# Layer 2's output product by Strassen's scheme, in one fused attention and two-layer MoE kernel

## The chip, the cores and the metric

The kernel runs on one core of a Trainium2 chip. The metric is device time in microseconds (us) for one execution. The kernel before took 905.86 us (median of 3 runs, 905.23 to 908.45). Engines: TensorE (PE; its weight loads are listed as PEld), VectorE (DVE), ScalarE (ACT), GpSimd (POOL) and SyncE (SP), which issues the DMAs one after the other. Matrix products accumulate in eight banks of PSUM.

## The reference

```python
attn_out = _attn_ref(q, k, v)                 # 4 x 8 heads x 576 x 64, causal window of 64
x = attn_out as (2304 tokens, 512)
# layer 1
xn = x / sqrt(mean(x*x) + 1e-6) * rms_g
g = xn @ w_gate;  h = g / (1 + exp(-g)) * (xn @ w_val)       # 512 x 1536 weights
x = h @ w_out                                                # 1536 x 512
# layer 2
gate = 1 / (1 + exp(-(x @ w2_gate)))
out = (gate * (x @ w2_val)) @ w2_out                         # (2304, 512)
```

All inputs and outputs are float32. A product is made of float16 parts: each operand is split into a high and a low part, and high x high, high x low and low x high are added up in PSUM, so that one product of a 128 x 128 weight piece is three matmuls.

## The kernel before

The 2304 tokens are six blocks of 384, and two blocks make a token pair (p = 0, 1, 2). The 1536 hidden columns are twelve tiles of 128 (f), and two tiles make a slab (s = 0 to 5). Weights come from DRAM in slabs j of 1 MB: j = 0 to 11 are gate and value (two for each hidden slab), j = 12 to 17 the output weights. A slab is loaded, its largest value is found (`w_max`), it is rounded (`w_conv`) and split into high and low part (`w_split`). For layer 2 a slab that was loaded early for its largest value is often loaded again later.

Already before the change, the gate and value products of layer 2 (all three pairs) and of pair 2 in layer 1 use Strassen's scheme (in Winograd's form) on 2 x 2 quadrants: `sums` makes the four weight combinations, which gives seven forms of a weight slab, `xform_items` makes seven forms of the tokens (four DVE subtractions, seven splits), and `moe_w(l, p, s)` runs seven products in place of eight for gate (m = 0) and seven for value (m = 1), each of six matmuls of 384 columns, and puts the quadrants together with ACT copies into PSUM banks and DVE adds (line 799). For layer 2 it then makes tanh (line 832), multiplies (line 840) and splits each of the four hidden quadrants into high and low part (ACT line 850, DVE line 851).

The output product of layer 2 is plain: `moe_o(1, blk, f)` runs, for each of the three 128-token tiles of a block, three matmuls of 512 columns (lines 636 to 638) with the hidden tile as the weight operand. After the last f, each token tile is scaled on ACT or DVE (lines 644, 646) and stored as 128 rows of 512 (line 648).

The seven token forms of a pair lie in `att` for pairs 0 and 2, and in places of `wl1` and `wl2` for pair 1 (`xform`). Layer 1's results `x2` stay in SBUF in the `xhl` buffers.

Program order is the list `main`: steps GV and W (gate and value), O (output product), with other work put beside them by `place`. The order in which each engine runs its instructions is then set wholly by the written list `ORDER`, unpacked in `arrange`: SP too takes its DMAs in that order. PSUM banks and buffers are taken from small lists (`room`, `take()`) in turn.

```python
for t in range(n // P):
    ts_ = slice(t * P, (t + 1) * P)
    T.matmul(o[t], lhsT=h[:, 0, ts_], rhs=wh, start=st, stop=False)
    T.matmul(o[t], lhsT=h[:, 0, ts_], rhs=wl, start=False, stop=False)
    T.matmul(o[t], lhsT=h[:, 1, ts_], rhs=wh, start=False, stop=en)
```

Of the kernel before, what the change touches and what calls it, by code (L numbers as in the profile page):

```python
# [35 lines left out]
CO = 6  # L36
AEND, REND = 7, 6
TRUNC = None
PLACE = {}
WIDE = set()  # L40
# [7 lines left out]
        10: (2, 28), 11: (2, 35), 12: (2, 42), 13: (2, 46), 14: (2, 50), 15: (1, 42), 16: (1, 48), 17: (1, 52)}  # L48
# [23 lines left out]
BANKS_OF = {"o": (0, 1, 2, 3), "gv": (4, 5), "at": (6, 7), "w": (4, 5, 6, 7), "any": (0, 1, 2, 3, 4, 5, 6, 7), "oat": (0, 1, 2, 3, 6, 7)}  # L72
# [35 lines left out]
def fused_kernel(ctx, tc, q, k, v, w_gate, w_val, w_out, rms_g, w2_gate, w2_val, w2_out, const16, const32, out, plan, asked):  # L108
# [5 lines left out]
    P = 128  # L114
# [15 lines left out]
    sp = Pool(ctx.enter_context(tc.tile_pool(name="sp", bufs=2)), plan, asked)  # L130
    ps = Pool(ctx.enter_context(tc.tile_pool(name="ps", bufs=1, space=bass.MemoryType.PSUM)), plan, asked)
# [88 lines left out]
    def wdst(layer, j):  # L220
        if layer == 0:
            return wl1[:, j * 2048:(j + 1) * 2048]
        home, k = DST2[j]
        return (wl1 if home == 1 else wl2)[:, k * KIB:(k + (7 if j < 12 else 4)) * KIB]
# [5 lines left out]
    def w_max(layer, j, n=1):  # L230
# [15 lines left out]
        top = 266 if layer == 1 and j < 12 else 268  # L246
# [45 lines left out]
    def w_l2_scale():  # L292
        pgv = pw[:, 1, 0:12].rearrange("p (s m) -> p s m", m=2)
        pf = small("pf", NG)
        V.tensor_tensor(out=pf, in0=pgv[:, :, 1], in1=pw[:, 1, 12:18], op=ALU.mult)
        cm = small("cm")
        V.tensor_reduce(out=cm, in_=pf, axis=AX.X, op=ALU.max)
        ic = small("ic")
        V.reciprocal(out=ic, in_=cm)
        V.tensor_scalar(out=hs2, in0=pf, scalar1=ic, scalar2=2.0 ** -21, op0=ALU.mult, op1=ALU.mult)  # L300
        V.tensor_scalar(out=tg2, in0=pgv[:, :, 0], scalar1=pt, scalar2=2.0 ** -39, op0=ALU.mult, op1=ALU.mult)
        V.tensor_scalar(out=ocm, in0=cm, scalar1=pt, scalar2=2.0 ** -32, op0=ALU.mult, op1=ALU.mult)
# [12 lines left out]
    def w_split(layer, j, half):  # L315
# [10 lines left out]
        if layer == 1 and j < 12:  # L326
            parts = [(x, d[:, 0:1024], d[:, 1792:2816]), (wraw(layer, j)[:, 0:768, 0].bitcast(F32), d[:, 1024:1792], d[:, 2816:3584])]
# [10 lines left out]

    def wo(layer, f):
        w = wdst(layer, 12 + f // 2)  # L340
        o = (f % 2) * 512
        return w[:, o:o + 512], w[:, 1024 + o:1536 + o]

# [260 lines left out]
    def moe_h(l, blk, f):  # L604
# [7 lines left out]
        hh[l, blk, f] = h  # L612
# [3 lines left out]
    def moe_o(l, blk, f):  # L616
        n = BLOCKS[blk]
        h = hh.pop((l, blk, f))
        if f == 0:
            ob[l, blk] = [bank("o") for _ in range(KC if l == 0 else n // P)]  # L620
        o = ob[l, blk]
        wh, wl = wo(l, f)
        st, en = f == 0, f == FC - 1
        if l == 0:
            hi, lo = h[:, 0, 0:n], h[:, 1, 0:n]
            for c in range(KC):
                cs = slice(c * P, (c + 1) * P)
                T.matmul(o[c][:, 0:n], lhsT=wh[:, cs], rhs=hi, start=st, stop=False)  # L628
                T.matmul(o[c][:, 0:n], lhsT=wh[:, cs], rhs=lo, start=False, stop=False)  # L629
                T.matmul(o[c][:, 0:n], lhsT=wl[:, cs], rhs=hi, start=False, stop=en)  # L630
            if (l, blk, f) in hbuf:
                room.append(hbuf.pop((l, blk, f)))
        else:
            for t in range(n // P):
                ts_ = slice(t * P, (t + 1) * P)
                T.matmul(o[t], lhsT=h[:, 0, ts_], rhs=wh, start=st, stop=False)  # L636
                T.matmul(o[t], lhsT=h[:, 0, ts_], rhs=wl, start=False, stop=False)  # L637
                T.matmul(o[t], lhsT=h[:, 1, ts_], rhs=wh, start=False, stop=en)  # L638
            room.append(hbuf.pop((l, blk, f)))
        if en and l == 1:  # L640
            for t in range(n // P):
                y = abuf("sm" if t % 2 else "vn", 0)
                if t % 2 == 0:
                    A.activation(out=y, in_=o[t], func=AF.Copy, scale=bx[blk // 2][2])
                else:
                    V.tensor_scalar(out=y, in0=o[t], scalar1=bx[blk // 2][2], scalar2=None, op0=ALU.mult)
                r0 = starts[blk] + t * P
                SY.dma_start(out=out[r0:r0 + P, :], in_=y)
            ob.pop((l, blk))
# [7 lines left out]
    def x1_a(blk):  # L657
        o = ob.pop((0, blk))
# [14 lines left out]
    sxs = {}  # L673
# [17 lines left out]
    def xform(l, p, q):  # L691
        if (l, p) == (1, 1):
            home, k = (wl1, 56 + 3 * q) if q < 5 else (wl2, 56 + 3 * (q - 5))
            a = home[:, k * KIB:(k + 3) * KIB]
        else:
            a = att[:, 2 * NMAX * q:2 * NMAX * (q + 1)].bitcast(F16)
        return a.rearrange("p (t k n) -> p t k n", t=2, k=2)

    def xform_items(l, p):
# [72 lines left out]
    def h5_home(f):  # L772
        s, i = divmod(f, 2)
        if s == 1:
            return abuf("sm", 0)[:, 0:NMAX]
        if s in (2, 3):
            if "x" not in h5:
                h5["x"] = six()
            return h5["x"][:, 2 * (s - 2) + i]
        o = {0: (40, 54), 4: (28, 29.5), 5: (31, 32.5)}[s][i]  # L780
# [6 lines left out]
    def product(pb, l, p, s, m, a, b, first):  # L787
        w, x = wdst(l, 2 * s + m), xform(l, p, b)
# [12 lines left out]
    def moe_w(l, p, s):  # L801
        be = bx[p][1][:, s:s + 1] if l else tgs[:, s:s + 1]
        th = {}
        for m in range(2):
# [13 lines left out]
            c = bank("w")  # L818
# [8 lines left out]
            for k, v in (((0, 0), a[:, 0:NMAX]), ((1, 1), x22), ((1, 0), x21), ((0, 1), c[:, 0:NMAX])):  # L827
# [13 lines left out]
                if held:  # L841
                    room.append(v)
                blk, f = 2 * p + j, 2 * s + i
                if not l and j:
                    hb = h5_home(f)
                else:
                    hb = hbuf[l, blk, f] = take()
                h = hb.bitcast(F16).rearrange("p (t n) -> p t n", t=2)
                sc = hs2[:, f // 2:f // 2 + 1] if l else 1.0
                A.activation(out=h[:, 0], in_=t, func=AF.Copy, scale=sc)  # L850
                V.scalar_tensor_tensor(out=h[:, 1], in0=t, scalar=sc, in1=h[:, 0], op0=ALU.mult, op1=ALU.subtract)
                hh[l, blk, f] = h
                room.append(t)


# [55 lines left out]
    late_o = [(b, f) for b in range(NB) for f in range(FC)]  # L911
    for p in range(NB // 2):
        for s in range(NG):
            main.append(("W", 1, p, s))
            for _ in range(4 if p else 2 if s else 0):
                oo(1, late_o[0][0], [late_o[0][1]])
                late_o.pop(0)
    for b, f in late_o:
        oo(1, b, [f])
# [27 lines left out]
    if True:  # L947
# [62 lines left out]
        lst += [load(12), load(13)] + conv(1, 12) + [load(14)] + conv(1, 13) + conv(1, 14)  # L1010
        for j in (4, 5, 6, 7, 8, 9, 10, 11, 15, 16, 17):
# [17 lines left out]
        after("W", 2, 5, [(("be",), lambda: x1_c(0))] + again(8, 9) + again(15))  # L1029
        after("O", 5, FC - 3, again(16, 17))  # L1030
# [19 lines left out]
        def do_o(l, b, f):  # L1050
            moe_o(l, b, f)
            if l == 0 and f == FC - 1:
                x1_a(b)

        def rooms():
# [3 lines left out]
            for i in range(2):  # L1059
                spare.append(abuf("vn", 0)[:, 0:NMAX])  # L1060
# [7 lines left out]
        def late_rooms():  # L1068
            for a in spare:
                k = [i for i, x in enumerate(room) if x is a]  # L1070
                room.pop(k[0])
            more_room(2)
            for home, k in ((wl2, 54), (wl1, 46)):
                room.append(home[:, k * KIB:k * KIB + 2 * NMAX].bitcast(F32))
# [200 lines left out]
```

## Time and profile before

| what | value |
|---|---|
| median of 3 runs | 905.86 us |
| the profiled execution | 904.97 us |
| its span | 903.2 us |
| PE, busy share of the span | 97% |
| DVE, busy share | 71% |
| ACT, busy share | 50% |
| DMA, mean rate | 84 GB/s |

The span runs from the first to the last recorded piece of work. A group of instructions is listed by its line and engine, with the tiles it writes and reads, the number of instructions, the engine's busy time in them and the mean duration of one. The chain of waits is followed back from the last instruction, at each step to what released it. Matmuls are pipelined, so their durations overlap; the distance of two starts is what one costs.

### The profile page before, as it was taken

The page shows a single profiled execution, that of the slowest core. Times are in us where ns is not written, and L with a number is a line of the kernel's source. Part 1 is how long each engine was busy: PE and PEld are TensorE (multiplying, and loading weights), DVE is VectorE, ACT ScalarE, POOL GpSimd, SP SyncE. Part 2 cuts the span into 40 slices and gives each one's busy share as a digit, 9 for nine tenths or more (in the row PEclk, how much of TensorE's full clock was granted, in tenths as well). Part 3 has the DMA queues.
Part 4 walks back from the last instruction along what each step waited for, and adds up shares of the span by engine and source line. Part 5 has one row for each costly group of instructions (what it writes and reads, how often), then busy time and mean ns, then how long its engine had stood idle before and what let it go on. Part 6 is the DMA issues. An engine that isn't in the chain of part 4 may idle for free.

```text
span 903.2 us, 14978 instructions
## 1 busy us (share of the span) xinstructions
PE 873.1 (97%) x6048; PEld 519.5 (58%) x6048; DVE 641.0 (71%) x1228; ACT 454.6 (50%) x965; POOL 30.8 (3%) x40
## 2 busy tenths in 40 slices
PE   4699999999999999999999999999999999999998
PEld 3566666666656666556666665555555555555543
DVE  6999998999999999999989577745342442223340
ACT  5867456547634555356565475454343432333420
POOL 0100000110020010100000000000000000000000
PEclk7799999999999999999999999999999999999999
DMA  9734534413684030001212122000000000000001
GB/s 345 276 135 167 205 129 165 158 65 118 226 309 159 13 106 25 1 1 48 94 48 94 47 94 94 1 1 1 24 12 1 24 1 1 36 1 36 1 35 47
DMA packets 19797, 75.44 MB, mean 84 GB/s; under 512 B 2320, under 2 KB 2704, under 8 KB 13712
## 3 DMA queue, kind: packets, MB, share of 16 engines
q1 hardware_dynamic: 19728, 74.49, 22.3%
q8 instruction: 47, 0.77, 0.3%
q14 instruction: 22, 0.18, 0.1%
HBM read 69.77 MB, written 4.72 MB: 82 GB/s over the span
## 4 chain that ended last, share of the span: by engine, by line
PE 78%; DVE 15%; DMA 4%; issue 1%; ACT 0%; POOL 0%; SPq 0%; DVEq 0%; ACTq 0%
PE bank L796 36%; PE bank L577 11%; PE bank L637 5%; PE bank L638 5%; PE bank L636 5%; PE bank L628 4%; PE bank L630 4%; PE bank L629 4%; DVE wmax L238 2%; DVE wl L332 2%; DMA wl<-in_moe_w_gate_dram 2%; DMA wl<-in_moe_w_out_dram 1%; PE bank L405 1%; PE bank L477 1%; DVE wl L267 1%
## 5 line engine op out<-in xcount | busy, mean ns | idle before, releaser
L796 PEld LDWEIGHTS <-wl 128*128 128x128 f16 x1944 | 190.2, 98 | 137.2 <-issue 1.2
L796 PE MATMUL bank<-att,wl 128*128 128x384 f16 x1440 | 252.6, 326 | 0.9 <-DVE att L709 0.9
L577 PE MATMUL bank<-xhl,wl 128*128 128x384 f16 x1152 | 197.4, 326 | 3.2 <-DVE th L590 1.7
L577 PEld LDWEIGHTS <-wl 128*128 128x128 f16 x1152 | 112.0, 98 | 77.5 <-issue 5.1
L809 ACT ACTIVATE bank<-bank 128x384 f32<-128x384 f32 x96 | 45.7, 476 | 121.3 <-PE bank L796 99.2
L330 ACT ACTIVATE wl<-wl,isc 128x1024 f16<-128x1024 f32 (+1 forms) x42 | 48.4, 1165 | 7.7 <-DVE isc L247 4.2
L589 ACT ACTIVATE th<-bank,tg 128x384 f32<-128x384 f32 x48 | 27.7, 576 | 44.8 <-PE bank L577 34.1
L421 ACT ACTIVATE sm<-sm,nm 128x128 f32<-128x128 f32 x96 | 37.3, 391 | 23.6 <-DVE nm L415 23.5
L238 DVE TENSOR_REDUCE wmax<-wl 128x1 f32<-128x1024 f32 x36 | 43.4, 1213 | 4.8 <-DMA wl<-in_moe_w_out_dram 2.0
L796 PE MATMUL bank<-wl 128*128 128x384 f16 x252 | 45.9, 326 | 0.0
L796 PE MATMUL bank<-wl,wl 128*128 128x384 f16 x252 | 45.2, 326 | 0.0
L265 ACT ACTIVATE wl<-wl 128x1024 f32<-128x1024 f32 x36 | 41.2, 1157 | 7.6 <-DMA wl<-in_moe_w_gate_dram 5.6
L636 PE MATMUL bank<-wl,xhl 128*128 128x512 f16 x111 | 42.1, 379 | 0.0
L637 PE MATMUL bank<-wl,xhl 128*128 128x512 f16 x111 | 42.1, 379 | 0.0
L638 PE MATMUL bank<-wl,xhl 128*128 128x512 f16 x111 | 42.1, 379 | 0.0
L840 DVE SCALAR_TENSOR_TENSOR xhl<-xhl,bank 128x384 f32<-128x384 f32 x18 | 9.9, 553 | 42.7 <-PE bank L796 42.7
L628 PE MATMUL bank<-wl,wl 128*128 128x384 f16 x120 | 39.2, 327 | 0.0
L629 PE MATMUL bank<-wl,wl 128*128 128x384 f16 x120 | 39.1, 326 | 0.0
L630 PE MATMUL bank<-wl,wl 128*128 128x384 f16 x120 | 39.1, 326 | 0.0
L630 PEld LDWEIGHTS <-wl 128*128 128x128 f16 x288 | 28.2, 98 | 18.6
L628 PEld LDWEIGHTS <-wl 128*128 128x128 f16 x288 | 28.1, 98 | 18.6 <-issue 1.0
L799 DVE TENSOR_TENSOR xhl<-xhl,bank 128x384 f32<-128x384 f32 x26 | 14.3, 552 | 34.3 <-PE bank L796 28.7
(339 smaller groups left out, 1540.3 us busy)
## 6 DMA issues: line engine op xcount, KB each, us to landing
wl<-in_moe_w_val_dram SPq DMA_DIRECT2D x16, 1024.0 KB, 5.0
wl<-in_moe_w_gate_dram SPq DMA_DIRECT2D x16, 1024.0 KB, 5.3
wl<-in_moe_w_out_dram SPq DMA_DIRECT2D x15, 1024.0 KB, 4.8
vn<-in_v_dram SPq DMA_DIRECT2D x27, 256.0 KB, 4.9
att<-in_k_dram SPq DMA_DIRECT2D x13, 384.0 KB, 5.4
att<-in_q_dram SPq DMA_DIRECT2D x17, 256.0 KB, 5.2
out_dram<-vn SPq DMA_DIRECT2D x12, 256.0 KB, 2.2
out_dram<-sm SPq DMA_DIRECT2D x6, 256.0 KB, 2.2
```

Of the source, the lines that this page charges most:

```text
L238: V.tensor_reduce(out=r1[:, i:i + 1], in_=wraw(layer, j + i)[:, :, 1].bitcast(F32), axis=AX.X, op=ALU.max, apply_absolute_value=True)
L265: A.activation(out=y.bitcast(F32), in_=hi.bitcast(F32), func=AF.Prelu, scale=2.0 ** -112, alpha=-2.0 ** 32)
L330: A.activation(out=hi, in_=y, func=AF.Copy, scale=sc)
L577: T.matmul(pb[:, 0:n], lhsT=w_, rhs=x_, start=(c == 0), stop=(c == m - 1))
L628: T.matmul(o[c][:, 0:n], lhsT=wh[:, cs], rhs=hi, start=st, stop=False)
L629: T.matmul(o[c][:, 0:n], lhsT=wh[:, cs], rhs=lo, start=False, stop=False)
L630: T.matmul(o[c][:, 0:n], lhsT=wl[:, cs], rhs=hi, start=False, stop=en)
L636: T.matmul(o[t], lhsT=h[:, 0, ts_], rhs=wh, start=st, stop=False)
L637: T.matmul(o[t], lhsT=h[:, 0, ts_], rhs=wl, start=False, stop=False)
L638: T.matmul(o[t], lhsT=h[:, 1, ts_], rhs=wh, start=False, stop=en)
L796: T.matmul(pb[:, 0:NMAX], lhsT=w_, rhs=x[:, t, kk], start=first and kk == n == 0, stop=kk == 1 and n == 2, skip_group_check=not first)
L809: A.activation(out=o[:, 0:NMAX], in_=i[:, 0:NMAX], func=AF.Copy)
```

## The change

- The output weights of layer 2 get Strassen forms as well: each of the slabs 12 to 17 now goes through `sums`, and its split covers 1792 columns in place of 1024.
- `moe_w` for layer 2 no longer splits four hidden quadrants; it makes seven forms of them (four DVE subtractions, seven splits on ACT and DVE).
- `moe_o` is left for layer 1 alone. The new `moe_p(p, ss, c)` runs layer 2's output product for one token pair, a group `ss` of two slabs, and one half c of 128 columns in each half of the output. It has seven products, each of 2 slabs x 3 matmuls of 384 columns, with the weight as weight operand, so that the result is transposed. The result of the first group goes from PSUM to an SBUF accumulator, those of the other two are added to it on DVE, and after the last group it is stored as 128 rows of 384. The host transposes the output array.
- Layer 1's results of blocks 2 to 5 are written to DRAM and fetched again. The token forms of pairs 1 and 2 are made in two staging places, written to DRAM, and fetched into `att`, the one place for forms that is left.
- Layer 2's products may take any of the eight PSUM banks (before, banks 4 to 7 for W and 0 to 3 for O).
- The steps stand as `PLAN2` has them, and `ORDER` is a new list.

```diff
+PLAN2 = [(0, 1, (0, 1), 2, 3, (2, 3), 4, 5, (4, 5)), (0, 1, 2, (0, 1), 3, 4, (2, 3), 5, (4, 5)), (0, 1, 2, (0, 1), 3, 4, (2, 3), 5, (4, 5))]
...
     def conv_rest(layer, i, split=True):
         r = [(("c", layer, i), lambda: w_conv(layer, i))]
-        if layer == 1 and i < 12:
+        if layer == 1:
             r.append((("q", layer, i), lambda: w_sums(i)))
...
         def split(q, x):
-            t = xform(l, p, q)
+            t = stage(q) if l and p else xform(q)
...
+            if l and p:
+                spill[p, 'f', q] = dp.tile([P, 2, 2, NMAX], F16, name=f"f{p}{q}")
+                SY.dma_start(out=spill[p, 'f', q], in_=t)
...
+        b11, b12, b21, b22 = (th[k] for k in ((0, 0), (0, 1), (1, 0), (1, 1)))
+        split(0, b11)
+        split(1, b21)
+        split(2, b22)
+        sub(b11, b12, b11)
+        split(4, b11)
+        sub(b12, b22, b12)
+        split(6, b12)
+        sub(b22, b22, b11)
+        split(5, b22)
+        sub(b21, b21, b22)
+        split(3, b21)
...
+    def moe_p(p, ss, c):
+        sc = bx[p][2]
+        first, last = ss[0] == 0, ss[-1] == NG - 1
+        def go(pb, a, b, st=False):
+            for s in ss:
+                w, o = wdst(1, 12 + s), a * 256 + c * P
+                x = hf[p, s, b].bitcast(F16).rearrange("p (t n) -> p t n", t=2)
+                wh, wl = w[:, o:o + P], w[:, 1792 + o:1792 + o + P]
+                for n, (w_, t) in enumerate(((wh, 0), (wh, 1), (wl, 0))):
+                    T.matmul(pb[:, 0:NMAX], lhsT=w_, rhs=x[:, t], ...)
+        def into(k, pb, fresh=False):
+            if fresh:
+                acc[p, c, k] = take()
+                A.activation(out=acc[p, c, k], in_=pb[:, 0:NMAX], func=AF.Copy, scale=sc)
+            else:
+                V.scalar_tensor_tensor(out=acc[p, c, k], in0=pb[:, 0:NMAX], scalar=sc, in1=acc[p, c, k], op0=ALU.mult, op1=ALU.add)
+        a, e = bank("w2"), bank("w2")
+        go(a, 0, 0, True)
+        go(e, 6, 6, True)
+        b = bank("w2")
+        copy(b, a)
+        go(a, 1, 1)
+        into((0, 0), a, first)
+        give((0, 0))
+        go(b, 5, 5)
+        d = bank("w2")
+        copy(d, b)
+        go(d, 4, 4)
+        go(b, 2, 3)
...
+        into((1, 0), b)
+        give((1, 0))
+        go(d, 3, 2)
+        into((0, 1), d, first)
+        give((0, 1))
...
-        place(xform_items(1, 1), pos["W", 1, 0, 4], w[1] - CO, post)
-        place(xform_items(1, 2), pos["W", 1, 1, 3], w[2] - CO, post)
+        for s, j in ((0, 14), (1, 16)):
+            place(again(j, j + 1), pos["W", 1, 0, s] + 1, pos["W", 1, 0, s] + 2, mid)
+        for p in (1, 2):
+            lst = [(("xx", p, j), lambda j=j: fetch_x(j)) for j in (2 * p, 2 * p + 1)] + xform_items(1, p)
+            place(lst, pos["W", 1, p - 1, 3], pos["W", 1, p - 1, 5], post)
+            place([(("xg", p, q), lambda p=p, q=q: fetch_form(p, q)) for q in (0, 6, 5, 1, 4, 3, 2)], ...)
```

The new `ORDER`, unpacked for layer 2: TensorE's list mixes the products of neighbouring steps. Below, W(p,s) is a gate and value step and P(p;s,s') an output group; a letter and a digit are one product of six matmuls (the PSUM bank's letter, and the number of the form that it reads, so b3 reads form 3). The passages are the one around the first output group of pair 0, with the end of W(0,1), and the one at the end of the kernel.

```
pair 0:  W(0,1) c4 c4 b3 b3 c2 c2 | P(0;0,1) a0 a0 a1 a1 | W(0,2) a0 | P(0;0,1) e6 e6 | W(0,2) a0 e6 | P(0;0,1) b5 b5 | W(0,2) e6 | P(0;0,1) d4 b3 d4 d2 b3
pair 2:  W(2,5) c4 c4 c2 c2 b3 | P(2;4,5) a0 | W(2,5) b3 | P(2;4,5) a0 e6 b5 b5 e6 a1 d4 d4 a1 d2 d2 b3 b3
```

DVE's list holds 202 instructions from the first of pair 0's layer-2 work to the last accumulation of its last group: 24 quadrant adds, 24 multiplications, 24 subtractions and 28 accumulations of 384 columns, 42 hidden splits, the rounding, sums and splits of the weight slabs 14 to 17, 11 token-form splits, 7 token-form subtractions and 10 small ones. For pair 1 there are 148, for pair 2 142. SP's list puts the fetches of pair 1's forms 5 and 2, and likewise those of pair 2, behind the first output store of the pair before.

## Rows read from the trace of the kernel before

**Rows 1.** The page's first part: busy time, share and instructions of each engine.

```profile
PE 873.1 (97%) x6048; PEld 519.5 (58%) x6048; DVE 641.0 (71%) x1228; ACT 454.6 (50%) x965; POOL 30.8 (3%) x40
```

**Rows 2.** Busy time by stretch: length, then each engine, granted clock, DMA share, GB/s.

```profile
0.00:60.00 60.00, 38.66 (x417) 27.84 (x418) 51.11 (x123) 41.72 (x115) 4.90 (x9) 0.80 0.69 259
60.00:400.00 340.00, 335.02 (x2774) 211.97 (x2772) 324.67 (x622) 187.72 (x443) 24.84 (x29) 1.00 0.35 127
400.00:540.00 140.00, 140.00 (x863) 84.32 (x862) 117.75 (x229) 85.15 (x146) 0.45 (x1) 1.00 0.19 68
540.00:860.00 320.00, 320.00 (x1814) 177.29 (x1812) 137.96 (x240) 133.55 (x252) 0.64 (x1) 1.00 0.04 16
860.00:899.50 39.50, 39.45 (x188) 18.12 (x185) 9.52 (x18) 5.79 (x11) 0.00 (x0) 1.00 0.11 40
899.50:903.20 3.70, 0.00 (x0) 0.00 (x0) 0.00 (x0) 0.69 (x1) 0.00 (x0) 1.00 0.19 71
```

**Rows 3.** What TensorE waited for from 60 to 904 us: us, times, longest.

```profile
PE bank L577 <- DVE th L590: 1.7, 3, 0.8
...
PE bank L529 <- DVE xhl L528: 0.5, 1, 0.5
```

**Rows 4.** Chain of waits in order of time: start, us, what.

```profile
101.29 31.20 PE bank L577 x192
...
880.02 0.22 PE bank L636
...
893.41 0.22 PE bank L638
```

**Rows 5.** Groups by line: busy, mean ns | idle before, releasers.

```profile
L809 ACT ACTIVATE bank<-bank 128x384 f32<-128x384 f32 x96 | 45.7, 476 | 121.3 <-PE bank L796 99.2 <-DVE xhl L840 8.0 <-DVE th L840 3.0
...
L267 DVE SCALAR_TENSOR_TENSOR wl<-wl,wl 128x1024 int32<-128x1024 int32 x27 | 33.0, 1221 | 3.8 <-ACT wl L265 3.6
L332 DVE SCALAR_TENSOR_TENSOR wl<-wl,isc,wl 128x1024 f16<-128x1024 f32 (+1 forms) x27 | 32.6, 1218 | 0.1
...
L266 DVE TENSOR_SCALAR wl<-wl 128x1024 int32<-128x1024 int32 x36 | 24.7, 687 | 0.3 <-DMA wl<-in_moe_w_gate_dram 0.3
...
L709 DVE SCALAR_TENSOR_TENSOR att<-xhl,sx,att 128x768 f16<-128x768 f32 x14 | 14.2, 1013 | 0.4 <-ACT att L708 0.4
...
L712 DVE TENSOR_TENSOR xhl<-xhl,xhl 128x768 f32<-128x768 f32 x12 | 11.4, 950 | 0.1
...
L308 DVE TENSOR_TENSOR wl<-wl 128x256 f32<-128x256 f32 x24 | 10.0, 419 | 0.0
...
L840 DVE SCALAR_TENSOR_TENSOR xhl<-xhl,bank 128x384 f32<-128x384 f32 x18 | 9.9, 553 | 42.7 <-PE bank L796 42.7
L850 ACT ACTIVATE xhl<-xhl,hs 128x384 f16<-128x384 f32 x16 | 9.6, 605 | 2.8 <-DVE xhl L840 2.8
...
L851 DVE SCALAR_TENSOR_TENSOR xhl<-xhl,hs,xhl 128x384 f16<-128x384 f32 x14 | 8.5, 612 | 4.8 <-ACT xhl L850 4.8
...
L644 ACT ACTIVATE vn<-bank,ga 128x512 f32<-128x512 f32 x12 | 8.2, 681 | 28.2 <-PE bank L638 28.2
...
L646 DVE TENSOR_SCALAR sm<-bank,ga 128x512 f32<-128x512 f32 x6 | 4.5, 750 | 26.0 <-PE bank L638 26.0
```

**Rows 6.** DVE's timeline where it works without a pause: start, us, instruction.

```profile
847.42 0.61 DVE L851 SCALAR_TENSOR_TENSOR wl<-xhl,hs,wl 128x384 f16<-128x384 f32 x1
847.95 0.61 DVE L851 SCALAR_TENSOR_TENSOR xhl<-xhl,hs 128x384 f16<-128x384 f32 x1
```

**Rows 7.** DMA issues: KB each, median us from issue to landing.

```profile
att<-in_k_dram SPq DMA_DIRECT2D x13, 384.0 KB, 5.4
...
out_dram<-vn SPq DMA_DIRECT2D x12, 256.0 KB, 2.2
```

**Rows 8.** Timeline of the end: the last matmul and the scaling of its result.

```profile
899.07 0.38 PE L638 MATMUL bank<-wl,xhl 128*128 128x512 f16 x1
899.54 0.69 ACT L644 ACTIVATE vn<-bank,ga 128x512 f32<-128x512 f32 x1 [3.85 <-PE bank L638]
```

More of the change, by code (lines that the diff above doesn't have):

```diff
@@ L245, in w_max @@
             return
[L246 removed]
+        top = 266 if layer == 1 else 268
         V.tensor_scalar(out=isc[:, layer, js].bitcast(I32), in0=p_.bitcast(I32), scalar1=-1.0, scalar2=float(top << 23), op0=ALU.mult, op1=ALU.add)
@@ L611, in moe_h, with moe_o @@
             h = xp.tile([P, 2, NMAX], F16, tag="hh", name="hh", bufs=LAG + 2)
-        hh[l, blk, f] = h
+        hh[blk, f] = h
         A.activation(out=h[:, 0, 0:n], in_=th[:, 0:n], func=AF.Copy)
         V.tensor_tensor(out=h[:, 1, 0:n], in0=th[:, 0:n], in1=h[:, 0, 0:n], op=ALU.subtract)
-    def moe_o(l, blk, f):
+    def moe_o(blk, f):
         n = BLOCKS[blk]
-        h = hh.pop((l, blk, f))
+        h = hh.pop((blk, f))
         if f == 0:
-            ob[l, blk] = [bank("o") for _ in range(KC if l == 0 else n // P)]
-        o = ob[l, blk]
-        wh, wl = wo(l, f)
-        st, en = f == 0, f == FC - 1
[L624 to L649, printed above, removed]
@@ new lines, in moe_o @@
+            ob[blk] = [bank("o") for _ in range(KC)]
+        o = ob[blk]
+        w = wdst(0, 12 + f // 2)
+        w0 = (f % 2) * 512
+        wh, wl = w[:, w0:w0 + 512], w[:, 1024 + w0:1536 + w0]
+        st, en = f == 0, f == FC - 1
+        hi, lo = h[:, 0, 0:n], h[:, 1, 0:n]
+        for c in range(KC):
+            cs = slice(c * P, (c + 1) * P)
+            T.matmul(o[c][:, 0:n], lhsT=wh[:, cs], rhs=hi, start=st, stop=False)
+            T.matmul(o[c][:, 0:n], lhsT=wh[:, cs], rhs=lo, start=False, stop=False)
+            T.matmul(o[c][:, 0:n], lhsT=wl[:, cs], rhs=hi, start=False, stop=en)
@@ L689, in x1_c, with xform, stage, fetch_form @@
         bx[p] = (px, be, ga)
[L691 to L696, printed above, removed]
-        return a.rearrange("p (t k n) -> p t k n", t=2, k=2)
+    def xform(q):
+        a = att[:, 2 * NMAX * q:2 * NMAX * (q + 1)].bitcast(F16)
+        return a.rearrange("p (t k n) -> p t k n", t=2, k=2)
+    def stage(q):
+        a = wl2[:, (56 + 3 * (q % 2)) * KIB:(59 + 3 * (q % 2)) * KIB]
+        return a.rearrange("p (t k n) -> p t k n", t=2, k=2)
+    def fetch_form(p, q):
+        SY.dma_start(out=xform(q), in_=spill[p, 'f', q])
     def xform_items(l, p):
@@ L842, in moe_w @@
                     room.append(v)
+                if l:
+                    continue
                 blk, f = 2 * p + j, 2 * s + i
[L844 to L847, printed above, removed]
+                hb = h5_home(f) if j else take()
+                if not j:
+                    hbuf[blk, f] = hb
                 h = hb.bitcast(F16).rearrange("p (t n) -> p t n", t=2)
-                sc = hs2[:, f // 2:f // 2 + 1] if l else 1.0
@@ new lines, in split, with sub @@
+        def split(q, x):
+            hf[p, s, q] = hb = take()
+            h = hb.bitcast(F16).rearrange("p (t n) -> p t n", t=2)
+            A.activation(out=h[:, 0], in_=x, func=AF.Copy, scale=sc)
+            V.scalar_tensor_tensor(out=h[:, 1], in0=x, scalar=sc, in1=h[:, 0], op0=ALU.mult, op1=ALU.subtract)
+        def sub(o, a, b):
+            V.tensor_tensor(out=o, in0=a, in1=b, op=ALU.subtract)
+        b11, b12, b21, b22 = (th[k] for k in ((0, 0), (0, 1), (1, 0), (1, 1)))
+        split(0, b11)
@@ new lines, in moe_w, with copy, give @@
+        split(1, b21)
[4 more added lines that the diff above has]
+        split(6, b12)
+        room.append(b12)
+        sub(b22, b22, b11)
+        room.append(b11)
+        split(5, b22)
+        sub(b21, b21, b22)
+        room.append(b22)
+        split(3, b21)
+        room.append(b21)
+    hf, acc = {}, {}
+    def moe_p(p, ss, c):
[7 more added lines that the diff above has]
+                for n, (w_, t) in enumerate(((wh, 0), (wh, 1), (wl, 0))):
+                    T.matmul(pb[:, 0:NMAX], lhsT=w_, rhs=x[:, t], start=st and s == ss[0] and n == 0, stop=s == ss[-1] and n == 2, skip_group_check=not st)
+        def copy(o, i):
+            A.activation(out=o[:, 0:NMAX], in_=i[:, 0:NMAX], func=AF.Copy)
+        def into(k, pb, fresh=False):
[4 more added lines that the diff above has]
+                V.scalar_tensor_tensor(out=acc[p, c, k], in0=pb[:, 0:NMAX], scalar=sc, in1=acc[p, c, k], op0=ALU.mult, op1=ALU.add)
+        def give(k):
+            if last:
+                y = acc.pop((p, c, k))
+                r0, t0 = k[0] * 256 + c * P, starts[2 * p + k[1]]
+                SY.dma_start(out=out[r0:r0 + P, t0:t0 + NMAX], in_=y)
+                room.append(y)
+        a, e = bank("w2"), bank("w2")
[11 more added lines that the diff above has]
+        go(b, 2, 3)
+        if first:
+            into((1, 0), e, True)
+            acc[p, c, (1, 1)] = take()
+            V.scalar_tensor_tensor(out=acc[p, c, (1, 1)], in0=d[:, 0:NMAX], scalar=sc, in1=acc[p, c, (1, 0)], op0=ALU.mult, op1=ALU.add)
+        else:
+            into((1, 0), e)
+            into((1, 1), e)
+            into((1, 1), d)
+        give((1, 1))
+        into((1, 0), b)
[3 more added lines that the diff above has]
+        give((0, 1))
+        if c:
+            for s in ss:
+                for q in range(7):
+                    room.append(hf.pop((p, s, q)))
@@ L1058, in rooms @@
             more_hh()
-            for i in range(2):
-                spare.append(abuf("vn", 0)[:, 0:NMAX])
+            for tag in ("sm", "vn"):
+                spare.extend(abuf(tag, 0)[:, 0:NMAX] for i in range(2))
             room.extend(spare)
@@ L1084, in step @@
                 return
+            if kind == "P":
+                for c in range(2):
+                    moe_p(b, f, c)
+                return
             if kind == "W":
```

187 lines of the change are left out of this document (96 added, 91 removed).

## The prediction, made before the changed kernel ran

> **What bounds the kernel now.** I read the page's first part, then the busy time by stretch, then TensorE's waits, then the chain of waits. TensorE is busy for 873.1 of 903.2 us [rows 1]. By stretch [rows 2] the reader is to see where the other 30 us lie: 21.3 us in the first 60, 5.0 us between 60 and 400, nothing from 400 to 860, and 3.75 us after the last matmul. What TensorE waited for after 60 us are five entries from 1.7 down to 0.5 us, 4.9 us together, all on DVE; the same view from 400 on names none [rows 3]. So layer 2, which the change rebuilds, is a row of matmuls without a gap.
>
> A busy share could still hide slack, since matmuls overlap. The chain shows what one costs: 192 matmuls of 384 columns in 31.20 us, 162.5 ns each, and 62 starts of 512 columns between 880.02 and 893.41 us, 216.0 ns each [rows 4]. That is 2.36 and 2.37 columns per ns, close to one column per cycle of the upper clock level (2.4 GHz), and the granted clock is 1.00 from 60 us on [rows 2]. The 863 matmuls of 400 to 540 times 162.5 ns are 140.2 us for 140.0 busy. The Trainium skill (Trainium Kernel Development and Optimization, Performance Expectations) calls matmul busy time a bad metric for exactly this overlap; if that held here, fewer columns would gain less than their share. The trace does not bear it out: issue is at the column rate, so columns removed are time removed, as long as TensorE stays fed.
>
> **The change part by part.**
>
> *Matmuls.* Removed: 6 blocks x 12 tiles x 3 token tiles x 3 = 648 of 512 columns, 648 x 0.2160 = 140.0 us. Added: 3 pairs x 3 groups x 2 halves x 7 products x 2 slabs x 3 = 756 of 384 columns, 756 x 0.1625 = 122.9 us. Net -17.1 us, all of it on the path. The 108 more weight loads lie beside matmuls, as 1814 do from 540 to 860, with PEld busy for 177 of 320 us [rows 2]; without cover a whole 162.5 ns more for each would be 17.5 us, but a load precedes every 384-column matmul already and does not widen the 162.5 ns.
>
> *Hidden forms.* For each of 18 slabs there are 3 more splits and 4 subtractions. DVE: 3 x 0.612 + 4 x 0.553 = 4.05 us; ACT: 3 x 0.605 = 1.8 us [rows 5]. Together 72.9 and 32.7 us.
>
> *Accumulations.* For each pair 28 on DVE (84 x 0.553 = 46.5 us) and 18 on ACT (54 x 0.476 = 25.7 us, by the copy's row). Gone are 6 scalings on DVE (4.5 us) and 12 on ACT (8.2 us) [rows 5]. So DVE gets about 115 us more in layer 2 and ACT 50, where DVE has been busy for 138 of 320 us and ACT for 134 [rows 2].
>
> *Weights.* Each output slab costs DVE 0.69 + 1.22 + 4 x 0.42 + 1.22 + 1.01 = 5.8 us with its sums [rows 5]. Slabs 14 to 17 now fall into pair 0 of layer 2: 23.3 us there. Before that stage DVE loses four slabs of 3.1 us and gains 2 x 2.7 us for slabs 12 and 13, 7 us less. This could give back part of the 5.0 us that TensorE idles from 60 to 400; the new order could as well lose as much again. Bounds -5 and +5; I take 0.
>
> *DVE in pair 0* is where the cover is thinnest. Its list of 202 instructions sums to 100 x 0.553 + 42 x 0.612 + 23.3 + 11 x 1.013 + 7 x 0.95 + 10 x 0.15 (an estimate for the small ones, whose columns are few) = 123.5 us, against 756 matmuls of 122.9 us. Row means overstate it: two splits of 0.61 us follow each other at 0.53 [rows 6], so 0.08 us less for each, 107 us, 87% of TensorE's time. Two stretches stand on either side: at 84% (400 to 540) TensorE lost nothing, at 95% (60 to 400) it lost 1.5% [rows 2]. Hence 0 to 1.8 us here; I take 1.0. Pairs 1 and 2 sum to some 85 and 81 us by the same rows, 66 to 69%.
>
> *The new wait at the groups.* A group's products wait for forms of the slab just before. From a quadrant's last matmul to its form there are a multiplication, a subtraction, an ACT split and a DVE split: 0.55 + 0.55 + 0.61 + 0.61 = 2.3 us [rows 5], more if DVE is behind, for its queue runs in order: other splits, sums and accumulations stand ahead, and the group's later products stand behind the waiting one on TensorE. Counted in the new list, TensorE has between W's last product and the first that reads form 6 five products at P(0;0,1), 4.9 us, and 2.9 to 3.9 us at the four other tight groups (two in pair 0, the last of pairs 1 and 2); the other four have over 10 us. No such wait stands in the trace. Below: 0, the wait for DVE in the stretch from 400 on. Above: one half slab's whole chain (2 adds, 4 multiplications, 4 subtractions, 7 splits: 9.8 us) less 2.9 us of cover, at nine groups, 62 us. I take 0.3 us at five groups, 1.5 us, near the lower end, since that row is of the same engines in the same stage.
>
> *Through DRAM.* Layer 1's four blocks of results, 0.79 MB each, and fourteen forms of 0.39 MB go out and come back, 17.3 MB; 24 stores of 192 KB replace 18 of 256 KB. DMA share there is 0.04 to 0.11 [rows 2]. A form's way back is between 2.2 us (a 256 KB store) and 5.4 us (a 384 KB load) [rows 7]; I take the load. What hides it: form 5 was last read by W(0,5), and counted in the new list 23 us of matmuls stand before W(1,0) reads it. Fetches of forms 5 and 2 queue on SP behind a store that waits for DVE, some 8 us ahead of the need. Taken as 0; without cover 5.4 us at each of two pair boundaries. Banks: any of eight for both steps, no cost.
>
> *The end.* Before, 3.75 us from the last matmul's end [rows 2] over a 0.69 us ACT step [rows 8] and a store. After, a 0.55 us DVE accumulation and a smaller store: 0.
>
> **Sum:** 904.97 (the profiled execution) - 17.1 + 1.0 + 1.5 = 890.4. The median lies 0.9 us above that execution, so I give 891.3, rounded 891.0.
>
> **The rivals.**
>
> *A: the new order loses in front.* The list is new for the whole kernel, and the first 400 us hold 26 us of idle time [rows 2], which a different order may enlarge. For it: DVE is 95% busy there. Against it: 7 us less to do on DVE. A quarter more idle time is 6.5 us: 897.5.
>
> *B: forms come late.* Before, pair 1 had places of its own; now one place serves every pair and must be read out first. The Trainium skill (same page, Best Practices) asks for double buffers so that DMA and compute overlap, and this change gives one up; no run here shows the cost yet. Twice 5.4 us: 891 + 10.8 = 902, no change. Against it: the 23 us of cover.
>
> *C: slower; the group heads run bare.* If DVE is behind at each head, nine groups wait on its queue. Faster turns to slower where a group loses (17.1 + 4.5) / 9 = 2.4 us on average; at half of the upper bound, 3.5 us, the time is 905.9 - 17.1 + 31.5 = 920. For it: the list gives as little as 2.9 us for a 2.3 us chain, and DVE in pair 0 is at 87 to 100%. Against it: pairs 1 and 2 leave DVE a third free, and TensorE's list fills in products of the next slabs.
>
> *D: the change doesn't take off what it says,* if a group's products, in which each matmul brings a new weight piece, issued slower than 162.5 ns. At 185 ns the gain is nil: 906. Layer 2's gate and value products are of that very form and do not.
>
> **How the numbers follow.** Forecast 0.70 (its own range 886 to 896), A 0.11, B 0.08, C 0.08, D 0.03. The range takes in the forecast, most of A, and stops before B: 885.5 to 899.5. About 0.5%, 4.5 us, is what a measurement here can tell from no change. Faster: forecast, A, and part of B, 0.85; same: the rest of B and most of D, 0.08; slower: C, 0.07.
>
> **What would show it.** Right: 756 matmuls in the new product's line at 162.5 ns, TensorE's waits from 540 on below 4 us, DVE busy for 250 us or more from 540 to the end, the granted clock at 1.00. Wrong: waits on the hidden forms of 2 us and more at the heads (C), on `att` behind a fetch (B), or over 27 us idle in the first 400 (A). The prediction falls if TensorE is idle for more than 10 us in layer 2.

## The result, and the profile after

The changed kernel took 890.69 us (median of 4 runs, 890.17 to 892.53) against 905.87 us before: ratio 0.9831 (95% interval 0.9807 to 0.9855), 15.2 us less. On a second chip it took 890.47 against 904.84 us, ratio 0.9841 (0.9828 to 0.9855), 14.4 us less. The forecast was 891.0 us.

The page's first part for the changed kernel, which answers to [rows 1]:

```profile
PE 859.7 (97%) x6156; PEld 531.2 (60%) x6156; DVE 759.7 (85%) x1462; ACT 505.9 (57%) x1067; POOL 26.6 (3%) x40
```

108 matmuls more, yet TensorE is busy for 13.4 us less; DVE is busy for 119 us more and ACT for 51. The prediction's rows add up to 115 for forms and accumulations and 23 - 7 for the weights, 131 in all, and to 50. The trace has less on DVE, where records back to back overlap [rows 6].

Busy time by stretch of the changed kernel, with the columns of [rows 2]:

```profile
0.00:60.00 60.00, 37.32 (x400) 27.34 (x401) 49.96 (x121) 39.88 (x104) 4.01 (x9) 0.74 0.72 267
60.00:400.00 340.00, 336.28 (x2775) 212.12 (x2774) 326.56 (x625) 188.28 (x453) 21.53 (x29) 1.00 0.37 128
400.00:520.00 120.00, 119.39 (x736) 71.77 (x735) 117.58 (x231) 77.95 (x129) 0.36 (x1) 1.00 0.28 95
520.00:645.00 125.00, 124.78 (x765) 74.67 (x764) 111.08 (x197) 80.89 (x145) 0.73 (x1) 1.00 0.32 111
645.00:770.00 125.00, 125.00 (x771) 75.23 (x769) 79.78 (x150) 61.15 (x123) 0.00 (x0) 1.00 0.16 56
770.00:887.10 117.10, 116.97 (x719) 70.04 (x716) 74.11 (x142) 57.71 (x117) 0.00 (x0) 1.00 0.04 12
887.10:890.70 3.60, 0.00 (x0) 0.00 (x0) 0.62 (x1) 0.00 (x0) 0.00 (x0) 1.00 0.49 176
```

The three stretches from 520 to 887 us hold the three token pairs of layer 2 nearly one by one. TensorE is full in all three; DVE is busy for 89% of pair 0, and for 64 and 63% of pairs 1 and 2. What TensorE waited for from 400 us on are two entries:

```profile
PE bank L788 <- ACT bank L801: 0.6, 1, 0.6
PE bank L889 <- DVE xhl L899: 0.2, 1, 0.2
```

The chain of waits, in order of time, shows the old gate and value products (line 788, 117 in 19.01 us) and the new output products (line 889, 48 in 7.80 us) at the same 162.5 ns for a matmul as the 384-column row of [rows 4]:

```profile
699.94 19.01 PE bank L788 x117
725.77 7.80 PE bank L889 x48
```

Two groups by line, to be held against line 840 of [rows 5], and the two DMA kinds that are new (KB, us to landing), against [rows 7]:

```profile
L899 DVE SCALAR_TENSOR_TENSOR xhl<-bank,ga,xhl 128x384 f32<-128x384 f32 x66 | 39.0, 612 | 13.5 <-PE bank L889 13.1
...
L791 DVE TENSOR_TENSOR xhl<-xhl,bank 128x384 f32<-128x384 f32 x33 | 17.7, 550 | 19.3 <-PE bank L788 16.5
```

```profile
f<-wl SPq DMA_DIRECT2D x14, 384.0 KB, 3.6
att<-f SPq DMA_DIRECT2D x14, 384.0 KB, 3.9
```

**Where the time came from.** The profiled execution after took 892.53 us (the slowest of its four), 12.4 less than the one before. Output product: 756 matmuls at 162.5 ns for 648 at 216.0 ns, -17.1. But TensorE's busy time after the first 60 us fell by only 834.47 - 822.42 = 12.05 us, from the sums of the stretches. Products of layer 1 in the two traces, from 60 us on (line 577 before, 573 after), show a first part of the difference:

```profile
L577 PE MATMUL bank<-xhl,wl 128*128 128x384 f16 x1098 | 188.5, 326 | 2.9 <-DVE th L590 1.7 <-DVE th L600 1.2
...
L573 PE MATMUL bank<-xhl,wl 128*128 128x384 f16 x1115 | 192.2, 326 | 3.1 <-DVE th L586 2.5 <-DVE wl L334 0.2 <-DVE th L596 0.2
```

The row of matmuls starts later, and 17 were left over, 2.8 us. The other 2.3 us are spread: the starts of the 756 new products lie 163.8 ns apart in the mean of the trace, which is 1.0 us, and most of the rest is in layer 1. Idle time after 60 us went from 5.0 to 4.7 us, the end from 3.7 to 3.6. That makes -17.1 + 2.8 + 2.3 - 0.3 - 0.1 = -12.4. The medians lie 15.2 us apart; no trace divides that difference.

### The profile page after: what moved, and what is told of

The parts are those of the page before. It is cut to its first block, busy times and chain, and to the rows that moved or that the text cites. A ratio compares the mean times of both kernels' runs of the same rounds, so it can differ in the third digit from the quotient of the medians.

```text
span 890.7 us, 15629 instructions
## 1 busy us (share of the span) xinstructions
PE 859.7 (97%) x6156; PEld 531.2 (60%) x6156; DVE 759.7 (85%) x1462; ACT 505.9 (57%) x1067; POOL 26.6 (3%) x40
## 4 chain that ended last, share of the span: by engine, by line
PE 75%; DVE 19%; ACT 2%; DMA 2%; issue 2%; SPq 0%; POOL 0%; DVEq 0%; ACTq 0%
PE bank L788 32%; PE bank L573 15%; PE bank L889 12%; PE bank L625 4%; PE bank L626 4%; PE bank L627 3%; PE bank L473 2%; PE bank L401 2%; DVE wl L269 1%; PE bank L434 1%; DVE wmax L240 1%; DVE wl L334 1%; DMA wl<-in_moe_w_out_dram 1%; DVE xhl L899 1%; DMA att<-in_k_dram 1%
## 5 line engine op out<-in xcount | busy, mean ns | idle before, releaser
L788 PE MATMUL bank<-att,wl 128*128 128x384 f16 x1944 | 329.6, 326 | 0.6 <-DVE att L700 0.4
L788 PEld LDWEIGHTS <-wl 128*128 128x128 f16 x1944 | 190.2, 98 | 127.0 <-issue 1.5
L573 PE MATMUL bank<-xhl,wl 128*128 128x384 f16 x1152 | 198.3, 326 | 3.1 <-DVE th L586 2.5
L573 PEld LDWEIGHTS <-wl 128*128 128x128 f16 x1152 | 111.4, 98 | 78.2 <-issue 5.7
L889 PEld LDWEIGHTS <-wl 128*128 128x128 f16 x756 | 73.9, 98 | 49.9 <-issue 1.1
L332 ACT ACTIVATE wl<-wl,isc 128x1024 f16<-128x1024 f32 (+1 forms) x48 | 53.9, 1143 | 20.6 <-DVE isc L249 12.5
L889 PE MATMUL bank<-xhl,wl 128*128 128x384 f16 x294 | 60.0, 326 | 0.1
L899 DVE SCALAR_TENSOR_TENSOR xhl<-bank,ga,xhl 128x384 f32<-128x384 f32 x66 | 39.0, 612 | 13.5 <-PE bank L889 13.1
L334 DVE SCALAR_TENSOR_TENSOR wl<-wl,isc,wl 128x1024 f16<-128x1024 f32 (+1 forms) x32 | 38.0, 1190 | 2.8 <-ACT wl L332 2.5
L627 PEld LDWEIGHTS <-wl 128*128 128x128 f16 x288 | 28.2, 98 | 19.0 <-issue 0.3
L625 PEld LDWEIGHTS <-wl 128*128 128x128 f16 x288 | 28.1, 98 | 18.0 <-issue 0.7
L626 PEld LDWEIGHTS <-wl 128*128 128x128 f16 x288 | 28.2, 98 | 17.2 <-issue 0.3
L625 PE MATMUL bank<-wl,wl 128*128 128x384 f16 x112 | 36.6, 326 | 0.0
L627 PE MATMUL bank<-wl,wl 128*128 128x384 f16 x112 | 36.5, 326 | 0.0
L626 PE MATMUL bank<-wl,wl 128*128 128x384 f16 x112 | 36.5, 326 | 0.0
L269 DVE SCALAR_TENSOR_TENSOR wl<-wl,wl 128x1024 int32<-128x1024 int32 x28 | 34.1, 1221 | 0.3
L791 DVE TENSOR_TENSOR xhl<-xhl,bank 128x384 f32<-128x384 f32 x33 | 17.7, 550 | 19.3 <-PE bank L788 16.5
```

What stands on the lines that cost most here:

```text
L269: V.scalar_tensor_tensor(out=y if (layer, j) in PACKED else hi, in0=y, scalar=3, in1=lo, op0=ALU.logical_shift_left, op1=ALU.bitwise_or)
L332: A.activation(out=hi, in_=y, func=AF.Copy, scale=sc)
L334: V.scalar_tensor_tensor(out=lo, in0=y, scalar=sc, in1=hi, op0=ALU.mult, op1=ALU.subtract)
L573: T.matmul(pb[:, 0:n], lhsT=w_, rhs=x_, start=(c == 0), stop=(c == m - 1))
L788: T.matmul(pb[:, 0:NMAX], lhsT=w_, rhs=x[:, t, kk], start=first and kk == n == 0, stop=kk == 1 and n == 2, skip_group_check=not first)
L889: T.matmul(pb[:, 0:NMAX], lhsT=w_, rhs=x[:, t], start=st and s == ss[0] and n == 0, stop=s == ss[-1] and n == 2, skip_group_check=not st)
```

## The experiments

All are compared with the changed kernel by way of runs of the kernel before on the same chip (904.33 to 905.40 us); "slower" and "faster" are against the control's 890.47.

**The changed kernel again.** 

> The changed kernel itself, for comparison on this chip. It took 890.7 us before. Theory (TensorE stays the bound, the change is worth its removed columns, 17.1 us, and the front of the new order gives some 3 us back): 889 to 892, that is 14 to 16 us below the kernel before. Rival (the gain is one of this chip's runs or of the front): outside of that.

Measured: 890.47 us, in the range. In its profile the granted clock is 1.00 in the first 40 us and 0.91 over the first 60, higher than in either profile above, and still only 395 matmuls are done by 60 us. So the late start does not need a low clock.

**The two fronts exchanged.** In both directions, what an engine had started in the first 60 us of the one kernel comes first in the other's list:

```diff
+    first = {k for f in FRONT.values() for k in f}
+    seq = [k for e in ENGINES for k in FRONT[e] + [k for k in seq if ops[k][0] == e and k not in first]]
     before = None
```

> The changed kernel, but what each engine had started in the first 60 us of the kernel before comes first, in the old order; all else in the new order. In the first two profiles TensorE's steady row of matmuls begins 2.7 us later after the change, and the granted clock of the first 60 us is 0.74 against 0.80. Theory F1 (that loss is the order's): 2 to 5 us faster than the changed kernel's 890.5. Rival F2 (it is a matter of the single execution, not of the order): within 1 us of it.

Measured: 895.19 us, 4.7 us slower (ratio to before 0.9893, 0.988 to 0.9907). Both theories failed: the old front starts earlier (412 matmuls by 60 us), but does not fit the new list behind it. TensorE was busy for 36.39 of the 40 us from 60 to 100, against 39.77 in the changed kernel.

> The other way round: the kernel before with the new order's first 60 us in front. F1: 2 to 5 us slower than the kernel before. F2: within 1 us of it.

Measured: 906.09 us against 904.89, ratio 1.0011 (1.0002 to 1.0021), 1.2 us slower; near F2 and just past it. Busy time by stretch of this kernel:

```profile
0.00:60.00 60.00, 35.48 (x394) 26.14 (x395) 49.05 (x119) 38.97 (x99) 4.02 (x9) 0.72 0.71 267
60.00:400.00 340.00, 336.25 (x2782) 212.77 (x2780) 324.56 (x620) 189.81 (x458) 25.30 (x29) 1.00 0.35 126
```

3.2 us are lost in the first 60 against [rows 2], and 1.2 us come back as less idle time behind. So the new front costs the old kernel about 1 us by the medians, and 2.5 us between the two profiled executions. (A first pair of versions, with the first 747 entries of the one program in the other's order, deadlocked and gave no time.)

**More columns for TensorE.**

```diff
         go(d, 3, 2)
+        go(d, 3, 2)
         into((0, 1), d, first)
```

> The changed kernel with the last of the seven products of each output group run twice (the output is then not the reference's): 108 matmuls of 384 columns more, with nothing more for DVE, ACT or the DMAs. Theory (TensorE's columns set the time in layer 2): 108 x 0.1625 = 17.6 us more, 908.2. Rival (the split and add chains on DVE set the pace in the new stage, and TensorE has slack there): less than 12 us more.

Measured: 907.34 us, 16.9 us slower, 156 ns for each added matmul. TensorE was busy for 379.52 of the 380 us from 520 on. The columns set the time in layer 2.

**Fewer columns for TensorE.** The output groups without their third term:

```diff
-                for n, (w_, t) in enumerate(((wh, 0), (wh, 1), (wl, 0))):
+                for n, (w_, t) in enumerate(((wh, 0), (wh, 1))):
```

> The changed kernel without the product low weight x high hidden in the output groups (the output is then less exact): 252 matmuls of 384 columns less, nothing else changed. If TensorE's columns alone set the time: 252 x 0.1625 = 41.0 us less than the changed kernel, 849.5. Theory after the two runs with doubled splits (DVE's list is full in pair 0 and packed at the heads elsewhere, so that TensorE and DVE bind together): well under half of it, 10 to 20 us less, 870 to 880.

Measured: 870.61 us, 19.9 us faster (ratio to before 0.9623, 0.9604 to 0.9642), half of the removed 41.0 us. Its three pairs by stretch:

```profile
520.00:640.00 120.00, 111.88 (x671) 65.36 (x670) 109.50 (x194) 79.62 (x143) 0.73 (x1) 1.00 0.32 114
640.00:755.00 115.00, 110.35 (x672) 65.45 (x671) 80.09 (x151) 61.84 (x124) 0.00 (x0) 1.00 0.16 56
755.00:868.00 113.00, 108.90 (x663) 64.59 (x661) 75.39 (x145) 58.33 (x119) 0.00 (x0) 1.00 0.06 21
```

TensorE now has gaps in all three, on lines of ACT and DVE alike, and DVE is no fuller in pairs 1 and 2 than 70%. With the written order as it is, only half of the removed columns paid. (This version is the fastest of all that ran, but its output product carries one term less of precision than that of either kernel.)

**More work for DVE between product and form.** A second, identical low-part split; an added instruction keeps its place behind the first:

```diff
             V.scalar_tensor_tensor(out=h[:, 1], in0=x, scalar=sc, in1=h[:, 0], op0=ALU.mult, op1=ALU.subtract)
+            if p == 0:
+                V.scalar_tensor_tensor(out=h[:, 1], in0=x, scalar=sc, in1=h[:, 0], op0=ALU.mult, op1=ALU.subtract)
```

> The changed kernel with each low-part split of the hidden forms of pair 0 done twice on DVE (42 instructions more, the same values): 22 to 26 us of DVE work more in a stretch of some 125 us in which DVE was busy for 111 us and TensorE for all. Theory (DVE has 14 us free in pair 0, and the order can use about half of them): 10 to 20 us slower. Rival by row means (DVE was full already): 22 to 26 us slower. Rival (the order leaves enough cover): under 5 us slower.

Measured: 915.32 us, 24.9 us slower: the rival by row means. Pair 0 of this kernel and what follows:

```profile
520.00:645.00 125.00, 110.67 (x651) 64.00 (x650) 114.08 (x201) 71.68 (x128) 0.64 (x1) 0.99 0.23 82
645.00:680.00 35.00, 30.56 (x176) 17.64 (x175) 24.07 (x43) 11.46 (x22) 0.00 (x0) 0.95 0.33 113
```

In these 125 us DVE is busy for 3 us more than without the doubling, and TensorE does 114 matmuls fewer. Of the 14 us in which DVE had been idle, 11 were not to be had.

> The same doubling in pairs 1 and 2 (84 instructions, 45 to 51 us of DVE work more), where DVE was busy for 80 of 125 and 74 of 117 us. Theory (a third of DVE is free there): under 5 us slower than the changed kernel. Rival C of the prediction (the chain on DVE at the group heads sets the pace): each head waits for two or more longer splits, 6 heads, 1 us or more each, and the slabs' own chains as well: 10 us slower or more.

Measured: 916.04 us, 25.6 us slower, half as much for each added instruction as in pair 0. The theory failed outright. Pairs 1 and 2:

```profile
645.00:770.00 125.00, 113.93 (x694) 67.54 (x692) 97.95 (x180) 59.60 (x120) 0.00 (x0) 1.00 0.12 39
770.00:907.00 137.00, 128.41 (x770) 75.70 (x769) 101.47 (x188) 59.58 (x120) 0.00 (x0) 0.99 0.05 18
```

TensorE loses 11.1 us in a stretch in which DVE is idle for 27. The page's first part, for the control and for this kernel:

```profile
PE 860.1 (97%) x6156; PEld 532.2 (60%) x6156; DVE 759.9 (85%) x1462; ACT 506.3 (57%) x1067; POOL 26.7 (3%) x40
...
PE 862.8 (94%) x6156; PEld 530.2 (58%) x6156; DVE 809.5 (89%) x1546; ACT 506.9 (55%) x1067; POOL 26.6 (3%) x40
```

DVE is busy for 49.6 us more, and the span grew by 24.1 us (914.0 against 889.9). So about half of the added work went into time in which DVE had been idle. In pair 0 it was 25.2 us more work and 23.0 us more span: almost nothing went there.

**More work for DVE behind the products.** The accumulations of pairs 1 and 2 twice, all but four:

```diff
                 V.scalar_tensor_tensor(out=acc[p, c, k], in0=pb[:, 0:NMAX], scalar=sc, in1=acc[p, c, k], op0=ALU.mult, op1=ALU.add)
+                if p > 0:
+                    V.scalar_tensor_tensor(out=acc[p, c, k], in0=pb[:, 0:NMAX], scalar=sc, in1=acc[p, c, k], op0=ALU.mult, op1=ALU.add)
```

> The changed kernel with each DVE accumulation of pairs 1 and 2 done twice (56 instructions more; the output is then not the reference's). The work goes to the same engine in the same stretch as in the run that doubled the hidden splits of pairs 1 and 2, which lost 0.30 us for each added instruction, but the accumulations stand behind the products, not between a product and the next group's forms. Theory (what lost time there was the chain from a product to the forms at the group heads): under 0.1 us each, less than 6 us slower than the changed kernel. Rival (DVE's list has no room, wherever the work stands): 0.3 us each, 17 us slower.

Measured: 911.80 us, 21.3 us slower: the rival's side. The edit adds 52 instructions and not 56, since four first sums (line 924 of the changed kernel) are made elsewhere; that is 0.41 us for each. DVE is busy for 31.7 us more, and the span is 20.3 us longer. So it is not the forms at the heads alone. What TensorE waited for from 500 us on (line 903 is the added accumulation, whose end gives back the PSUM bank):

```profile
PE bank L890 <- DVE xhl L903: 5.2, 2, 4.0
PE bank L789 <- ACT bank L802: 3.1, 2, 2.9
PE bank L890 <- DVE wl L903: 2.4, 1, 2.4
PE bank L789 <- DVE xhl L903: 2.1, 1, 2.1
```

Why DVE's idle third can be spent only in part shows in what DVE itself waited for in pairs 1 and 2 of the control (from 645 us on), the first four entries:

```profile
DVE xhl L791 <- PE bank L788: 16.5, 9, 4.8
DVE xhl L899 <- PE bank L889: 10.3, 11, 1.6
DVE xhl L833 <- PE bank L788: 8.5, 5, 4.0
DVE th L855 <- ACT th L854: 7.6, 2, 6.1
```

It waits for products that are still to come, and for ACT, and works in bursts between. An instruction put into a burst delays what follows it in the fixed list, and TensorE waits for that, as the lines above show. Which of the two kinds of wait, forms or banks, weighs more was not separated further.

**Small doses.** The second low-part split once more, in pairs 1 and 2 and for one of the seven forms only (`if p > 0 and q == 2:`, then `q == 3`).

> A seventh of the doubling that cost 25.5 us: in pairs 1 and 2 only the split of form 2 is done twice (12 instructions, 7.7 us of DVE work). Form 2 is read last of the seven by an output group. If the loss is in proportion to the work (0.30 us for each instruction): 3.6 us slower than the changed kernel's 890.5. If the written order holds a margin that has to be used up first: under 1 us. If the loss goes by how soon a form is needed: under 1 us here, and more in the run with form 3.

Measured: 892.61 us, 2.1 us slower (ratio to before 0.9871, 0.9849 to 0.9893).

> The same with form 3 (12 instructions, 7.7 us), which is made last of the seven. In proportion: 3.6 us slower. A margin: under 1 us. By how soon a form is needed: 4 us or more, six groups with 0.64 us for each of two slabs.

Measured: 891.59 us, 1.1 us slower (0.9853, 0.9838 to 0.9869). Neither interval is clear of the control's. That a form's urgency decides is not borne out: the one that is made last cost no more. A proportional 3.6 us fits neither median, though the first interval still holds it. The traces are clearer: DVE is busy for 7.1 us more in both, while TensorE's waits from 520 us on are 1.1 us with form 2 and 0.2 us with form 3, as in the control, and the spans 0.9 and 0.0 us longer. So 7 us of work were taken in almost wholly. Exactly where this margin ends stays open.

**The group heads closer to their slab.** TensorE's list alone is changed. At the last groups of the three pairs it becomes (here pair 2):

```diff
-W(2,5) b3 | P(2;4,5) a0 | W(2,5) b3 | P(2;4,5) a0 e6 b5 b5 e6 a1 ...
+W(2,5) b3 b3 | P(2;4,5) a0 a0 e6 e6 b5 b5 a1 ...
```

> The changed kernel with another order on TensorE alone, at the last groups of the three pairs: the group follows its slab in one piece and reads form 6 right after form 0, two products (1.95 us) after the slab's last product, where the order has three to four. Theory (a chain of 2.3 us and more from product to form stands there, and the written order just covers it): 1 to 2 us lost at each, 3 to 6 us slower. Rival (there is spare cover): within 1 us of the changed kernel.

Measured: 898.06 us, 7.6 us slower (0.9927, 0.9912 to 0.9941), somewhat over the theory. By stretch TensorE is idle for 4.2 us around pair 0's last group (625 to 655 us) and 1.7 us around pair 1's (745 to 775), where the control has none, and for no more than the control at pair 2's: there the slab ends on other products, and form 6 did not come closer to its own. So it is two heads, not three. The first three entries of what TensorE waited for from 500 us on are the splits' lines (854 on ACT, 855 on DVE):

```profile
PE bank L889 <- DVE wl L855: 2.1, 3, 1.1
PE bank L889 <- ACT wl L854: 1.4, 1, 1.4
PE bank L889 <- ACT hh L854: 1.2, 1, 1.2
```

**The forms fetched late.** SP's list alone is changed (here at the end of pair 0; likewise at the end of pair 1):

```diff
-fetch 1/5, fetch 1/2, store, spill 2/4, spill 2/5, six stores
+store, spill 2/4, spill 2/5, six stores, fetch 1/5, fetch 1/2
```

> The changed kernel with another order on SP alone: the fetches of forms 5 and 2 for pairs 1 and 2 stand behind all output stores of the pair before, not behind the first. In the changed kernel's trace they are issued some 12 us before the first product that reads them; so they would go out some 15 us later, after the need. Theory (rival B's price holds, but the order's cover hides it): one wait of 5 to 9 us at each of two boundaries, 10 to 18 us slower. Rival (the way through DRAM has more cover than that, or TensorE's list lets others pass): under 3 us slower.

Measured: 907.52 us, 17.0 us slower, the upper end of the theory. TensorE's largest wait, and the stretch around the first of the two:

```profile
PE bank L788 <- DMA att<-f: 11.0, 2, 7.0
```

```profile
645.00:650.00 5.00, 0.00 (x0) 0.00 (x0) 0.00 (x0) 0.00 (x0) 0.00 (x0) 0.80 1.01 341
650.00:655.00 5.00, 4.79 (x16) 2.32 (x17) 0.00 (x0) 0.47 (x1) 0.00 (x0) 0.52 0.10 36
655.00:660.00 5.00, 5.00 (x33) 3.00 (x32) 1.05 (x3) 2.72 (x6) 0.00 (x0) 1.00 0.00 0
```

TensorE is idle for 7 us and then starts 16 matmuls in 5 us, at a granted clock of 0.52 (near the lower of its two levels, 1.2 GHz), before it is back at the full row. The timeline gives the price:

```profile
650.21 12.03 PE L788 MATMUL bank<-att,wl 128*128 128x384 f16 x59 [7.03 <-DMA att<-f]
```

At 162.5 ns from start to start 59 matmuls take 9.75 us; here it was 12.03, so 2.3 us were lost on top of the wait. At the second boundary the wait was 4.0 us, and 1.5 us more were lost in the same way.

## Why the prediction was right

**The matmuls (-17.1 us): right, and they carry the result.** The new products issue at 162.5 ns in an unbroken run (163.8 ns in the mean), and more columns cost 156 ns for each matmul. Rival D is out.

**The new waits (+2.5 us taken): too large.** TensorE waited 0.2 us in layer 2 for what the trace names, 0.4 us of idle time in all from 520 to 887, and 0.6 us just before. The written order covers the heads as counted: where two heads came one to two products closer, 4.2 and 1.7 us were lost, so the chain of 2.3 us and more is real and the cover is what hides it.

**The front (0 taken): too small.** Rival A's mechanism happened in part: the new front starts TensorE's steady row about 3 us later. Idle time in the first 400 us hardly moved (26.3 us before, 26.4 after, under the 27 that the prediction had set as the sign of A); what came short is work, 17 matmuls or 2.8 us in the profiled execution. In the kernel before, the new front costs 1.2 us by the medians.

So two terms were off by 1 to 3 us each, in opposite directions. That forecast and median differ by only 0.3 us is luck, and so is the rounding of 891.3 to 891.0; the profiled executions lie 12.4 us apart, where the sum had 14.6.

**DVE in pair 0: busy time right, its meaning wrong.** I corrected the row means' 123.5 us to 107, and the trace has 111 of 125 us. But the correction was used to argue that there was room, from stretches that were 84 and 95% full. The changed kernel itself lost nothing there, but there was hardly any room left: 42 added splits cost 24.9 us. A full DVE is not the whole reason, for pairs 1 and 2 lose by added work too, at 64% busy. One of the signs also missed: DVE is busy for 246 us from 540 us to the end (91.9 + 79.8 + 74.1 + 0.6) and not 250; from 520 us, where pair 0 of layer 2 starts, it is 266. An accumulation took 0.61 us rather than the 0.55 of line 840, 5 us over all, beside the path.

**Rival C: the mechanism is close, the argument against it fell.** I held against it that pairs 1 and 2 leave DVE a third free. They do, and 84 added instructions still cost 25.6 us, half of the time that they took on DVE. What kept the change from C is the order's cover at the heads; the share of free time on DVE does not tell how much more it would bear.

**Rival B: the price was too low, the cover held.** The timeline of the changed kernel has the last two fetches for pair 1, forms 5 and 2, from 632.92 us on, and the first product of pair 1 that reads form 5 after 644.69:

```profile
632.92 0.43 SPq L688 DMA_DIRECT2D att<-f  x1
...
644.69 3.58 PE L788 MATMUL bank<-att,wl 128*128 128x384 f16 x21
```

A fetch landed in 3.9 us. Without that cover a boundary costs 8.5 us in the mean of the medians, rather than 5.4; in the trace it was 9.3 and 5.5 us, wait and low clock together. Here the Trainium skill's advice to double-buffer (Trainium Kernel Development and Optimization, Best Practices) was given up without a wait that the trace shows, and the late fetches show what it would have cost without some 12 us in the list.

**DRAM, banks, the end:** 0, as taken; 3.6 us after the last matmul for 3.75.

## What to carry to other kernels

Where matmuls issue at the column rate and no wait is listed, a scheme that removes an eighth of the columns is worth nearly an eighth (here 14.4 to 15.2 us of 17.1), if the list of the other engines has been fitted to it: count the cover in the written order at each place where a product must wait for a chain. The idle share of an engine that feeds such a list is not all room, since it waits for products that are still to come: of added work, nearly all was taken in at 7 us, about half at 50 us, and almost none where the engine was 89% busy. So try added instructions before counting on it. Offsetting small terms can make a forecast look finer than it is; check each against its own stretch.

## What the runs showed of the hardware that I had not expected

A wait of 7 us on TensorE was followed by 5 us at a granted clock of 0.52, and 2.3 us were lost after the wait had ended. Shorter waits that follow each other did the same: in the run with doubled accumulations, TensorE lost 6.1 us of busy time in pair 1, but did 61 matmuls fewer than the changed kernel, 9.9 us by the column rate.

```profile
645.00:770.00 125.00, 118.88 (x710) 70.40 (x709) 87.70 (x163) 60.08 (x121) 0.00 (x0) 0.97 0.13 44
```

In the run with pair 0's splits doubled the clock was 0.95 from 645 to 680 us, where TensorE was busy for 30.56 of 35 us. So a wait's price in this kernel can be more than its length. It need not be: with the heads closer to their slab, 4.2 us of idle time from 625 to 655 us left the clock at 1.00.
